# A fused attention and mixing kernel: a third buffer for the weights' raw words, 57 tile slots, and a new order of all steps

## The chip, the cores and the metric

The kernel runs on one core of a Trainium2 chip. The metric is device time in microseconds of the whole program. An engine is named by its short name in the rows: PE is TensorE (and PEld its queue of weight loads), DVE is VectorE, ACT is ScalarE, POOL is GpSimd, and SP is the queue that issues the DMAs.

## The reference, cut to what matters

Three blocks follow one another on 4 batches of 768 positions and 384 channels (8 heads of 48). All inputs are float32.

```python
def _attn_ref(q, k, v, alpha):
    for t in range(S):
        state = alpha[:, :, t, :, None] * state + np.einsum('bhd,bhe->bhde', k[:, :, t], v[:, :, t])
        y[:, :, t] = np.einsum('bhd,bhde->bhe', q[:, :, t], state)

def _moe_ref(x, U, V, w_ch1, w_ch2):          # U 768x32, V 32x768, w_ch1 384x1536
    h = x.transpose(0, 2, 1) @ U @ V
    u = x + h.transpose(0, 2, 1)
    return u + np.maximum(u @ w_ch1, 0.0) @ w_ch2

def _moe2_ref(x, w_theta, w_tok_r, w_tok_i, w_ch):
    theta = x @ w_theta
    zr, zi = x * np.cos(theta), x * np.sin(theta)
    y = np.einsum('ts,bsd->btd', w_tok_r, zr) + np.einsum('ts,bsd->btd', w_tok_i, zi)
    u = x + y
    return u + np.maximum(u @ w_ch, 0.0)
```

## The kernel before

**Attention** is worked off in 16 pairs of heads (4 per batch), each in 6 chunks of 128 positions. A pair's inputs `al`, `kk`, `qq`, `vv` are loaded by `att_load` (L189, L190). `prep_k` and `prep_q` make running products of the decay on DVE (the scans L197 and L206) and multiply them into k and q (L199 and L207, on DVE for pairs 0 to 3 and, with one exception, on POOL from pair 4 on). On PE the pair then passes through `att_pe`: transposes of k (L273, copied out by ACT as `kt`), scores A (L252), increments of the state D (L284), the product within the chunks (L305) and that with the earlier state (L313). For pairs 0 to 3 ACT copies the scores out (L259) and POOL masks them (L260); for the later ones DVE does both (L263). L295 on DVE is the scan over the chunks' states, L315 on ACT copies the result Y to `xp`, and SP moves it into the batch's X by DMA (L373). The squares (L234, L235, on ACT) are sums for a flag that is looked at when the program ends; once they are done, the pair's `al` and `G` are free.

**The second block** first mixes positions through U and V. For batch 0 `rank_columns` does so by blocks of 128 channels, as soon as the pairs of a block are there: transposes (L437), ACT's copy (L438), the product with U (L444), `gc` by ACT and DVE (L448, L449), and then two `lift`s of it: x plus the product with V in PSUM (L420, L421), split into a high and a low part `uh` by ACT and DVE (L158, L159), and X written back (L423). The other batches use `rank` (transposes L391). Then come the layers: `expand` is 9 products of 128x384 (L542 to L544) with `wh` and `wl`, the high and low part of a weight, followed by relu on ACT (L563) and the low part on DVE (L564); `contract` is 9 products into `acc`, two steps behind. The third block has theta, a mixing over positions (L724) and a channel product, from tiles that are made in the same manner.

**Weights** come as 64-bit words. `load64` (L169) brings the raw words into a tile `raw` of the pool `rw`, and `conv` puts float32 together from them in three DVE instructions (L466, L468, L470). For the layers' weights ACT then makes the high part (L481) and DVE the low part (L484), which is left until the next conversion is under way.

**Order.** There is no scheduler: every group of steps is a generator, `ORDER` is a string of letters, and each letter advances one generator by a step. What it issues goes into the engines' queues in this order, and every engine takes its own queue in order. D loads a pair, P prepares one, A is a step of `att_pe`, Q a pair's squares, U the load of U and V, L a step of the layers' weights, 0 to 2 a step of a column of `rank_columns`, K of `rank`, M and N of the layers for the two halves of the positions, T of the third block's weights, X loads X again, H is theta, G mixing, C the channel product, F the flag. A step whose input is missing drives the other generator until it is there.

**Memory.** Tiles of 128x768 live in `SLOTS` slots; a tile takes the slot that became free longest ago (`take`, `done_with`), and the DMA or instruction that first writes it waits for the slot's last reader.

Of the kernel before, what the change touches and what calls it, by code (L numbers as in the profile page):

```python
# [24 lines left out]
NF = FF // 128  # L25
HT = S // 2
RANK = 32
SLOTS = 59
LAG = 2

LATE = 0
# [3 lines left out]


ORDER = """
PAAAAAAQAAPUAAAPAUAAAADPAAUUA0U0UPUAAAALPAA0LALALAP1A01AA1PLL1AA0LAAA22A012L2LA2LLLMMD12ALLLMLMMNNLLNMLNLLNLNL
MLNLLLM1MNQLMNMLNLQLAPNNMLQMLMLLLMLLMMMDMMPNMMDMPMAAAAQDAUAQPANPAUNAAAAAAAQPNPNAADAAAAAAAPNANQAAKKNKKKKPNKKKAA
AAPKAANAAADAAKKNNKMQADMAMQMPMMPMMAK2PMMAAMMAAPDAAKMMMPQMMANAAAAQAPADAAMTMMPALAAQAAATAMKPQMNAMNAMDNKNNPKNKKAAAA  # L40
ADPANPNANQLANTKNAAAAAAPKKNNKTAANKNNAANNNAAA0AKKNNATKLMKTKNKMKNQMMMTMTKKMMNMNKMNKKMMMKKNKMTXKMMMKMNMTKNMMNNNNND
MMMNNNTKNMNNNNKNNNNMLMTMMHMTTMMTNTMTTNNMHHNNNTNMMNHMHNHTNFLTPNHNMHNTTTNMTHLHTNMMLMNHMMTTMNNTTTNMNHTPTNHHXNTTT1
MNNGMGGGNHHHGGHG2TTHTGGGHTHGTGGGGTGGTGGGGHGGGHPHHGGGTTHTGNGGGHGGGGHMLFGGGGGHFGQGGHXHHHGGGHGGGGCCGHGHTGLGCGHGGG
HHGGGHGNPFHGGGG0HGLHGHGGCQAHGGGCGCMH0HGHGGGLGHGGHGGHHGDGGTHHHGGGGCHCGGHGGHGGKHLAHGHCDGLGHGLGHGGGHCGGCHGGGHFHHG
GGGHHGCGGHGGHGHHHGGGGGHFGGGGGHCGGCXGHGCGGHGGHKCHLGCGGGGGXGGCCCCCCHAGGLPCCC
"""


# [14 lines left out]
def linear_attention_moe_kernel(ctx, tc, aT, kT, qT, vP, vT, U, V4, w1, w2, wth, wtr, wti, wch, out):  # L63
# [4 lines left out]
    pools = {}  # L68

    @contextmanager  # L70
    def work(slots, name):
        old = dict(pools)
        with ExitStack() as es:
            pools["big"] = es.enter_context(tc.tile_pool(name=f"big{name}", bufs=slots))
            pools["sml"] = es.enter_context(tc.tile_pool(name=f"sml{name}", bufs=3))
            pools["rw"] = es.enter_context(tc.tile_pool(name=f"rw{name}", bufs=2))
            pools["ps"] = es.enter_context(tc.tile_pool(name=f"ps{name}", bufs=8, space=bass.MemoryType.PSUM))
            yield
        pools.clear()
        pools.update(old)  # L80
# [8 lines left out]

    fast = ExitStack()  # L90
    fast.enter_context(work(SLOTS, "f"))
    dr = ctx.enter_context(tc.tile_pool(name="dr", bufs=1, space=bass.MemoryType.DRAM))


    free, home = {"on": True, "s": list(range(SLOTS)), "p": list(range(8))}, {}

# [9 lines left out]
    def T(name, dt=F32):  # L106
        return take("s", name, 768, dt)
# [4 lines left out]
    def done_with(*ts):  # L112
        for t in ts:
            if t.tensor.name in home:
                kind, i = home.pop(t.tensor.name)
                free[kind].append(i)
# [4 lines left out]
    def two(t):  # L121
        return t.rearrange("p (a b) -> p a b", a=2)
# [29 lines left out]
    def split(src, hi, lo, e_hi=None, e_lo=None):  # L152
        if e_hi is pool:
            pool.tensor_scalar(out=hi, in0=src, scalar1=1.0, scalar2=0.0, op0=ALU.mult, op1=ALU.add)
        elif e_hi is dve:
            dve.tensor_copy(hi, src)
        else:
            act.copy(hi, src)  # L158
        (e_lo or dve).tensor_tensor(out=lo, in0=src, in1=hi.bitcast(F32), op=ALU.subtract)  # L159

    def load64(*srcs):
        r = pools["rw"].tile([128, 1536], I32, tag="raw", name="raw")
        o = 0
        for x in srcs:
            n = x.free_size() * 2
            d = r[:, o:o + n]
            if len(x.shape) == 3:
                d = d.rearrange("p (a b) -> p a b", a=x.shape[1])
            sync.dma_start(d, x.bitcast(I32))  # L169
            o += n  # L170
        return r, o // 2
# [289 lines left out]
    def conv(raw, put):  # L461

        r, n = raw
        lo, hi = (r[:, 0:2 * n].rearrange("p (n t) -> p n t", t=2)[:, :, i] for i in range(2))
        t = T("cv", I32)[:, 0:n]
        dve.tensor_scalar(out=t, in0=hi, scalar1=3, scalar2=0x3FFFFFFF, op0=ALU.logical_shift_left, op1=ALU.bitwise_and)  # L466
        yield n * 0.6
        dve.scalar_tensor_tensor(out=t, in0=hi, scalar=-0x40000000, in1=t, op0=ALU.bitwise_and, op1=ALU.bitwise_or)  # L468
        yield n * 1.25
        dve.scalar_tensor_tensor(out=t, in0=lo, scalar=29, in1=t, op0=ALU.logical_shift_right, op1=ALU.bitwise_or)  # L470
        put(t.bitcast(F32))
        yield n * 1.25

    def load_w12():

        lows = []

        def put(n, W):
            def high(v):
                h, l = T("wh", F32R), T("wl", F32R)  # L480
                act.copy(h, v)  # L481

                def low():
                    (dve if BY_W[n] == "V" else pool).tensor_tensor(out=l, in0=v, in1=h.bitcast(F32), op=ALU.subtract)  # L484
                    done_with(v)
                    W.extend((two(h)[:, i], two(l)[:, i]) for i in range(2))

                lows.append(low)
                load(n + 2)

            return high

        first, second = [[(f, w, W) for f in range(0, NF, 2)] for w, W in ((w1, W1), (w2, W2))]
        todo = first[:1] + [x for y in zip(first[1:], second) for x in y] + second[-1:]
        raws = {}

        def load(n):
            if n < len(todo):
                f, w, W = todo[n]
                raws[n] = load64(w[f:f + 2].rearrange("f p n -> p f n"))  # L500

        for n in range(2):
            load(n)
        yield 0
        for n in range(len(todo)):
            g = conv(raws.pop(n), put(n, todo[n][2]))
            yield next(g)
            yield next(g)
            if lows:
                lows.pop()()  # L510
            yield next(g)
        lows.pop()()
# [110 lines left out]
    def load_second():  # L623
        def by():
            return dve if BY_T[len(WT) + min(len(CH), KD - 1)] == "V" else pool

        def put_thch(v):
            v = two(v)
            pool.tensor_scalar(out=v[:, 0], in0=v[:, 0], scalar1=INV2PI, scalar2=0.0, op0=ALU.mult, op1=ALU.add)
            for i, W in ((0, TH), (1, CH)):  # L630
                t = two(T("wt", F32R))
                split(v[:, i], t[:, 0], t[:, 1], e_lo=by())
                W.append(t)
            done_with(v)

        def put_tok(key):
            def put(v):
                hi, lo = T("wkh", F32R), T("wkl", F32R)
                split(v, hi, lo, e_lo=by())
                done_with(v)  # L640
                WT[key] = (hi, lo)
            return put

        todo = [((wth[j], wch[j]), put_thch) for j in range(KD)]
        todo += [((w[s],), put_tok((n, s))) for s in range(NC) for n, w in (("r", wtr), ("i", wti))]
        raws = {}

        def load(i):
            if i < len(todo):
                raws[i] = load64(*todo[i][0])  # L650

        load(0)
        load(1)
        yield 0
        for i, (_, put) in enumerate(todo):
            yield from conv(raws.pop(i), put)
            load(i + 2)

    def load_x1(b):
        if b < B - 1:  # L660
# [158 lines left out]
    att_load(0, 0)  # L819
    att_load(0, 1)  # L820
    lw, lu = load_w12(), load_uv()
    next(lu)
    att_load(0, 2)
# [132 lines left out]
    def checked():  # L956
        while late or len(done) < B * NP:
# [3 lines left out]
    done, ready = [], [(0, 0)]  # L961
    gens = {"D": loads(), "P": preps(), "A": products(), "Q": squared(), "U": lu, "L": lw, "K": others(),
            "M": layers(0), "N": layers(1), "T": load_second(), "X": back(), "H": angles(), "G": mixing(),
            "C": channels(), "F": checked()}
    gens.update((str(j), mixed(j)) for j in range(KD))
# [7 lines left out]
    with tc.If(fine[0] < 1):  # L973
        xg = dr.tile([B * NP, 96, S], F32, name="xg")
        x1g = dr.tile([B, KD, 128, S], F32, name="x1g")
        with work(1, "ga"):
            att_any(xg)
        flat = xg.rearrange("(b p) c t -> b (p c) t", b=B).rearrange("b (k c) t -> b k c t", k=KD)
        with work(30, "g1"):
            drain(load_uv())  # L980
            W1.clear()
            W2.clear()
            drain(load_w12())
            with tc.For_i(0, B) as i, inner(24, "g2"):
                X["any"] = [T(f"X{j}") for j in range(KD)]
                for j in range(KD):
                    sync.dma_start(X["any"][j], flat[bass.ds(i, 1), j].rearrange("a p t -> (a p) t"))
                drain(rank("any"))
                drain(mlp("any"))
                drain(finish())  # L990
                for j in range(KD):
                    sync.dma_start(x1g[bass.ds(i, 1), j].rearrange("a p t -> (a p) t"), X["any"][j])
# [68 lines left out]
```

## Time and profile before

| what | value |
|---|---|
| time, median of 3 runs | 682.81 us (682.65 to 682.84) |
| time of the profiled execution | 682.58 us |
| its span, first to last instruction | 680.8 us |
| busy: PE, PEld, DVE, ACT, POOL | 661.6, 638.4, 396.9, 250.5, 143.5 us |
| mean granted clock of PE | 0.999 |
| read from HBM, written | 49.40 MB, 8.26 MB |

The span is that of the profiled execution, and busy times are within it. PE is busy for 97% of the span. A busy time counts an instruction from its start to its modelled end, so the drain of one matmul can lie over the start of the next; where the text counts work on PE, it counts from start to start.

### The profile page before, as it was taken

How to read it: one execution, taken by the hardware profiler on the slowest of the kernel's cores; microseconds unless marked ns; L12 is line 12 of the kernel's file. 1: busy time of each engine (PE TensorE's matmuls, PEld its weight loads, DVE VectorE, ACT ScalarE, POOL GpSimd, SP SyncE). 2: the span in 40 equal slices, each digit the busy share in tenths (PEclk: the TensorE clock that was granted, in tenths of full speed). 3: DMA queues.
4: the chain of work that ended last, by engine and by line, in shares of the span. 5: the costliest groups of instructions: out<-in, count | busy, mean ns of one | idle time of the engine just before them, and what ended most of it. 6: DMA issues, size and time to landing. Idle time of an engine off the chain costs nothing.

```text
span 680.8 us, 11581 instructions
## 1 busy us (share of the span) xinstructions
PE 661.6 (97%) x4766; PEld 638.4 (94%) x4766; DVE 396.9 (58%) x615; ACT 250.5 (37%) x519; POOL 143.5 (21%) x123
## 2 busy tenths in 40 slices
PE   6889999999999999999999999999999999999996
PEld 4678999989999999999999999999999999999996
DVE  8998887868656566444333755657642363454233
ACT  3555352542534333242212444323441343244120
POOL 4550012222222132010100412415230121122010
PEclk9999999999999999999999999999999999999999
DMA  8735555333716330250100412412020000000002
GB/s 319 259 125 192 174 172 163 120 107 106 243 37 198 105 106 20 65 186 0 47 1 1 162 48 93 162 48 92 1 70 36 0 36 1 36 24 12 25 36 86
DMA packets 24077, 63.20 MB, mean 93 GB/s; under 512 B 2896, under 2 KB 6864, under 8 KB 24016
## 3 DMA queue, kind: packets, MB, share of 16 engines
q1 hardware_dynamic: 24016, 62.39, 27.6%
q8 instruction: 39, 0.64, 0.4%
q14 instruction: 22, 0.18, 0.1%
HBM read 49.40 MB, written 8.26 MB: 85 GB/s over the span
## 4 chain that ended last, share of the span: by engine, by line
PE 91%; DVE 5%; DMA 1%; issue 1%; POOL 1%; ACT 1%; SPq 0%; DVEq 0%; ACTq 0%; POOLq 0%
PE mx L724 22%; PE acc L542 8%; PE h L542 7%; PE acc L544 7%; PE acc L543 7%; PE h L543 7%; PE h L544 7%; PE Y L313 3%; PE A L252 3%; PE Y L305 3%; PE th L544 2%; PE ch L542 2%; PE ch L544 2%; PE th L542 2%; PE th L543 2%; PE ch L543 2%
## 5 line engine op out<-in xcount | busy, mean ns | idle before, releaser
L564 DVE SCALAR_TENSOR_TENSOR hh<-h,hh 128x384 fp32r<-128x384 f32 x96 | 53.0, 555 | 104.5 <-ACT hh L563 104.3
L542 PE MATMUL acc<-hh,wh 128*128 128x384 f32 x288 | 97.7, 339 | 0.0
L542 PE MATMUL h<-uh,wh 128*128 128x384 f32 x288 | 97.3, 338 | 0.0
L544 PE MATMUL acc<-hh,wl 128*128 128x384 f32 x288 | 96.4, 335 | 0.0
L544 PE MATMUL h<-uh,wl 128*128 128x384 f32 x288 | 96.4, 335 | 0.0
L543 PE MATMUL h<-uh,wh 128*128 128x384 f32 x288 | 96.4, 335 | 0.0
L543 PE MATMUL acc<-hh,wh 128*128 128x384 f32 x288 | 96.3, 335 | 0.0
L563 ACT ACTIVATE hh<-h 128x384 fp32r<-128x384 f32 x96 | 46.7, 490 | 97.9 <-PE h L544 96.8
L724 PE MATMUL mx<-wkh,zh 128*128 128x384 f32 x288 | 74.8, 340 | 0.0
L724 PE MATMUL mx<-wkl,zh 128*128 128x384 f32 x288 | 73.4, 335 | 0.0
L724 PE MATMUL mx<-wkh,zl 128*128 128x384 f32 x288 | 73.2, 335 | 0.0
L542 PEld LDWEIGHTS acc<-hh,wh 128*128 128x128 f32 x288 | 54.1, 188 | 1.0
L542 PEld LDWEIGHTS h<-uh,wh 128*128 128x128 f32 x288 | 54.1, 188 | 0.8
L543 PEld LDWEIGHTS h<-uh,wh 128*128 128x128 f32 x288 | 54.1, 188 | 0.3 <-DVE uh L159 0.3
L543 PEld LDWEIGHTS acc<-hh,wh 128*128 128x128 f32 x288 | 54.1, 188 | 0.0
L544 PEld LDWEIGHTS acc<-hh,wl 128*128 128x128 f32 x288 | 54.1, 188 | 0.0
L544 PEld LDWEIGHTS h<-uh,wl 128*128 128x128 f32 x288 | 54.1, 188 | 0.0
L724 PEld LDWEIGHTS mx<-wkh,zl 128*128 128x128 f32 x288 | 52.1, 188 | 0.0
L724 PEld LDWEIGHTS mx<-wkl,zh 128*128 128x128 f32 x288 | 51.9, 188 | 0.2 <-POOL wkl L159 0.2
L724 PEld LDWEIGHTS mx<-wkh,zh 128*128 128x128 f32 x288 | 50.9, 188 | 0.0
L199 POOL TENSOR_TENSOR kk<-kk,G 128x767 f32<-128x767 f32 x12 | 21.9, 1829 | 111.4 <-DVE G L197 87.5
L691 ACT COPY xc<-x1t 128x384 f32<-128x384 f32 x24 | 11.5, 479 | 82.2 <-PE x1t L685 82.2
(135 smaller groups left out, 1195.5 us busy)
## 6 DMA issues: line engine op xcount, KB each, us to landing
raw<-in_w SPq DMA_DIRECT2D x12, 768.0 KB, 4.4
al<-in_aT SPq DMA_DIRECT2D x15, 384.0 KB, 3.9
kk<-in_kT SPq DMA_DIRECT2D x15, 384.0 KB, 4.3
qq<-in_qT SPq DMA_DIRECT2D x15, 384.0 KB, 5.2
vv<-in_vP SPq DMA_DIRECT2D x16, 291.0 KB, 5.1
raw<-in_wtr SPq DMA_DIRECT2D x6, 768.0 KB, 4.3
raw<-in_wti SPq DMA_DIRECT2D x6, 768.0 KB, 4.4
out<-ot SPq DMA_DIRECT2D x24, 192.0 KB, 1.9
```

Source lines behind the costliest of these rows:

```text
L199: (dve if BY_K[b * NP + p] == "V" else pool).tensor_tensor(out=k[:, x:y - 1], in0=k[:, x:y - 1], in1=G[:, x:y - 1], op=ALU.mult)
L252: pe.matmul(ts[h][:, j * C:(j + 1) * C], k[r, c], q[r, c], start=True, stop=True)
L305: pe.matmul(t[64 * h:64 * h + n, o], v[:, c * 96 + h * D:c * 96 + h * D + n], ms[g][h][:, j], start=(j == 0), stop=(c == 0), skip_group_ch ...
L313: pe.matmul(t[64 * h:64 * h + D, o], st[64 * h:64 * h + 64, :, c - 1], q[64 * h:64 * h + 64, c * C:(c + 1) * C], start=False, stop=True, s ...
L542: pe.matmul(out, a[0], b[0], start=first, stop=False)
L543: pe.matmul(out, a[0], b[1], start=False, stop=False)
L544: pe.matmul(out, a[1], b[0], start=False, stop=last)
L563: act.activation(h[:, 0], t[:, 0:HT], ACTF.Relu)
L564: dve.scalar_tensor_tensor(out=h[:, 1], in0=t[:, 0:HT], scalar=0.0, in1=h[:, 0].bitcast(F32), op0=ALU.max, op1=ALU.subtract)
L691: act.copy(xc, xt[:, 0:DM])
L724: pe.matmul(ACC[b, j][hf][:, 0:HT], z[:, i, c], w[:, hf * HT:(hf + 1) * HT], start=f, stop=l)
```

## The change

Three things. The pool of raw words gets three buffers instead of two in the main part of the program, and both generators that load weights begin three loads ahead instead of two. There are 57 tile slots instead of 59, which pays for the buffer. And `ORDER` is a new string. Every instruction of the program is still there, in the same number on each engine.

```diff
-SLOTS = 59
+SLOTS = 57
...
 ORDER = """
-PAAAAAAQAAPUAAAPAUAAAADPAAUUA0U0UPUAAAALPAA0LALALAP1A01AA1PLL1AA0LAAA22A012L2LA2LLLMMD12ALLLMLMMNNLLNMLNLLNLNL
...
+AAAAPAAAAPAUPUAAAAAAPAAAAU0UUPU0AUAAALQPL0ALADAAA1LPA01AAPLA00A122LLA1AA221122LLMQLALNMNLNAALLALMLLLMLLMMMLLLN
...
-            pools["rw"] = es.enter_context(tc.tile_pool(name=f"rw{name}", bufs=2))
+            pools["rw"] = es.enter_context(tc.tile_pool(name=f"rw{name}", bufs=3 if name == "f" else 2))
...
                 lows.append(low)
-                load(n + 2)
+                load(n + 3)
...
-        for n in range(2):
+        for n in range(3):
             load(n)
...
         load(0)
         load(1)
+        load(2)
         yield 0
         for i, (_, put) in enumerate(todo):
             yield from conv(raws.pop(i), put)
-            load(i + 2)
+            load(i + 3)
```

What this does to the queues is shown at three places. The first is SP's queue after the first copies to X. X_336 (X_342 in the new kernel) and X_472 (X_475) are channel blocks 1 and 2 of batch 0, the copies to them here come from pairs 1 and 2, and al, kk, qq, vv belong to pair 4. Before:

```order
L373 DMA X_336<-xp 48x768
L189 DMA al<-in_aT 128x768
L189 DMA kk<-in_kT 128x768
L189 DMA qq<-in_qT 128x768
L190 DMA vv<-in_vP 128x582
L169 DMA raw<-in_w 128x2x768 x2
L373 DMA X_336<-xp 48x768
L373 DMA X_336<-xp 16x768
L373 DMA X_472<-xp 32x768
L169 DMA raw<-in_w 128x2x768
```

After:

```order
L373 DMA X_342<-xp 48x768
L169 DMA raw<-in_w 128x2x768 x3
L373 DMA X_342<-xp 48x768
L373 DMA X_342<-xp 16x768
L373 DMA X_475<-xp 32x768
L189 DMA al<-in_aT 128x768
L189 DMA kk<-in_kT 128x768
L189 DMA qq<-in_qT 128x768
L190 DMA vv<-in_vP 128x582
L169 DMA raw<-in_w 128x2x768
```

Pair 4's four loads moved from ahead of the raw loads to behind them and behind pair 2's three copies to X, and three raw loads stand together.

The second place is the start of ACT's queue, from pair 0's second copies of the scores to pair 3's `tb`; the two rows of L234 and L235 are pair 0's squares. Before:

```order
L259 COPY Am_84<-A 128x384 x2
L234 ACTIVATE junk,sq<-al 128x768
L235 ACTIVATE junk,sq<-G 128x767
L315 COPY xp<-Y 112x384 x2
L231 COPY tb<-tt 128x288
```

After, the same stretch, and then the place between pair 2's copies of Y and pair 3's `tb`:

```order
L259 COPY Am_84<-A 128x384 x2
L315 COPY xp<-Y 112x384 x2
L231 COPY tb<-tt 128x288
```

```order
L438 COPY xs<-xt 128x384 x2
L315 COPY xp<-Y 112x384 x2
L234 ACTIVATE junk,sq<-al 128x768
L235 ACTIVATE junk,sq<-G 128x767
L231 COPY tb<-tt 128x288
L274 COPY kt<-kT 128x384
L274 COPY kt<-kT 128x256
L259 COPY Am_83<-A 128x384 x2
```

The squares moved from behind pair 0's scores, where they were the only thing to do, to the place ahead of pair 3's `tb`, `kt` and scores.

The third place is PE's queue from the scores of pair 4 on; X_243 (X_241) is channel block 0. Before:

```order
L252 MATMUL A<-qq,kk 128x128 x12
L284 MATMUL D<-vv,kt 64x48 x10
L437 MATMUL xt<-ident,X_472 128x128 x6
L420 MATMUL h<-X_243,ident 128x384
L421 MATMUL h<-v_400,gc 128x384
L420 MATMUL h<-X_336,ident 128x384
L421 MATMUL h<-v_400,gc 128x384
L444 MATMUL g<-xs,uf 128x128 x6
L305 MATMUL Y<-Am_85,vv 64x128
```

After:

```order
L252 MATMUL A<-qq,kk 128x128 x12
L284 MATMUL D<-vv,kt 64x48 x10
L444 MATMUL g<-xs,uf 128x128 x6
L420 MATMUL h<-X_342,ident 128x384
L421 MATMUL h<-v_390,gc 128x384
L420 MATMUL h<-X_342,ident 128x384
L421 MATMUL h<-v_390,gc 128x384
L420 MATMUL h<-X_475,ident 128x384
L421 MATMUL h<-v_390,gc 128x384
L420 MATMUL h<-X_475,ident 128x384
L421 MATMUL h<-v_390,gc 128x384
L542 MATMUL h_721<-uh,wh 128x384
```

The transposes L437 and two lifts now stand ahead of pair 4's scores, the four other lifts follow one another, and h_721 is the first of five expands that come before pair 4's L305; in the kernel before there were two expands between L305 and L313, with two lifts behind them.

## Rows read from the trace of the kernel before

**Rows 1.** Busy time by stretch (us from start; engines' us, instructions; clock; DMA share, GB/s).

```profile
25.00:65.00 40.00, 34.53 (x367) 28.05 (x364) 36.88 (x50) 21.37 (x50) 16.34 (x13) 1.00 0.52 174
65.00:675.00 610.00, 609.29 (x4202) 596.06 (x4200) 337.97 (x530) 218.10 (x445) 117.39 (x82) 1.00 0.24 80
```

**Rows 2.** TensorE's waits: line, releaser: us in total, times, longest us.

```profile
PE Y L305 <- POOL Am L260: 2.6, 5, 0.9
PE xt L437 <- DMA X<-xp: 2.1, 2, 1.6
```

**Rows 3.** Who waited for the tile raw, whole run (us, times).

```profile
  DVE cv L466: 0.3, 1
```

**Rows 4.** SP's queue in time: start us, us, instruction, count.

```profile
25.99 0.58 SPq L189 DMA_DIRECT2D al<-in_aT  x1
...
34.83 1.79 SPq L373 DMA_DIRECT2D X<-xp  x3
```

**Rows 5.** DMA issues: count, KB each, us to landing (page; X at 140 to 148 us).

```profile
al<-in_aT SPq DMA_DIRECT2D x15, 384.0 KB, 3.9
...
X<-xp SPq DMA_DIRECT2D x2, 144.0 KB, 2.8
```

**Rows 6.** VectorE in time: start us, us, instruction, count [idle before <-releaser].

```profile
13.84 1.76 DVE L206 TENSOR_TENSOR_SCAN al<-al,starts 128x768 f32<-128x768 f32 x1
...
35.99 0.57 DVE L466 TENSOR_SCALAR cv<-raw 128x768 int32<-128x768 int32 x1 [0.30 <-DMA raw<-in_w]
...
38.66 2.06 DVE L197 TENSOR_TENSOR_SCAN G<-al,ends 128x767 f32<-128x767 f32 x1
...
40.94 0.76 DVE L295 TENSOR_TENSOR_SCAN S<-D,tb 128x288 f32<-128x288 f32 x1
41.73 0.30 DVE L449 TENSOR_TENSOR gc<-g,gc 32x128 fp32r<-32x128 f32 x1
...
42.29 2.63 DVE L206 TENSOR_TENSOR_SCAN al<-al,starts 128x768 f32<-128x768 f32 x1
...
63.94 0.95 DVE L484 TENSOR_TENSOR wl<-cv,wh 128x768 fp32r<-128x768 f32 x1
```

**Rows 7.** ScalarE in time.

```profile
12.29 0.89 ACT L234 ACTIVATE junk<-al 128x768 bf16<-128x768 f32 x1
...
14.06 0.19 ACT L235 ACTIVATION_READ_ACCUMULATOR junk<-G 128x1 f32 x1
...
36.75 1.64 ACT L259 COPY Am<-A 128x384 f32<-128x384 f32 x4
...
55.36 0.48 ACT L423 COPY X<-h 128x384 f32<-128x384 f32 x1 [0.62 <-DVE uh L159]
```

**Rows 8.** POOL in time.

```profile
37.38 4.14 POOL L260 TENSOR_SCALAR_AFFINE_SELECT Am<-Am 128x384 f32<-128x384 f32 x4 [1.72 <-ACT Am L259]
41.49 1.81 POOL L199 TENSOR_TENSOR kk<-kk,G 128x767 f32<-128x767 f32 x1
44.99 2.13 POOL L207 TENSOR_TENSOR qq<-qq,al 128x768 f32<-128x768 f32 x1 [1.69 <-DVE tt L228]
```

**Rows 9.** TensorE in time, 25 to 70 us.

```profile
42.35 1.34 PE L313 MATMUL Y<-qq,S 64*48 64x128 f32 x20
...
65.05 0.34 PE L544 MATMUL acc<-hh,wl 128*128 128x384 f32 x1
```

**Rows 10.** Busy time in one stretch, columns as in the first group.

```profile
42.35:64.70 22.35, 21.23 (x189) 17.32 (x189) 19.99 (x30) 11.10 (x26) 3.08 (x2) 1.00 0.33 107
```

**Rows 11.** TensorE in time, 138 to 150 us.

```profile
140.54 1.33 PE L313 MATMUL Y<-qq,S 64*48 64x128 f32 x20
...
147.53 1.03 PE L391 MATMUL xt<-ident,X 128*128 128x128 f32 x6 [0.19 <-DVE Am L263]
```

**Rows 12.** ScalarE in time, 138 to 150 us.

```profile
141.92 0.48 ACT L315 COPY xp<-Y 112x384 f32<-112x384 f32 x1 [0.18 <-PE Y L313]
```

**Rows 13.** The queue of TensorE's weight loads: waits, us, times, longest us.

```profile
PEld Y L313 <- DVE S L295: 2.5, 8, 0.5
```

More of the change, by code (lines that the diff above doesn't have):

```diff
@@ L37 @@
 ORDER = """
-PAAAAAAQAAPUAAAPAUAAAADPAAUUA0U0UPUAAAALPAA0LALALAP1A01AA1PLL1AA0LAAA22A012L2LA2LLLMMD12ALLLMLMMNNLLNMLNLLNLNL
[L39 to L45, printed above, removed]
+AAAAPAAAAPAUPUAAAAAAPAAAAU0UUPU0AUAAALQPL0ALADAAA1LPA01AAPLA00A122LLA1AA221122LLMQLALNMNLNAALLALMLLLMLLMMMLLLN
+L0MMLMLNMLQMNLLLDNNLLNMLMLLNLMLMMMTMLPMMNMPAMDMPNAANQAAAQUANDPAPNAAAAAAQQADNUAPAPAAAAAQAAPNNKKNKKKKAKDKAAKAAQP
+AKKNNANPDNLAKADNMMPMMAUAAAAPAPLMAAMK1M2QAQAAAAKMMDAPMPMAMMMAAAKMMMAAAAAMPAAAQAAAQKAKDMKAPMMPMMMKTKNKQAKNDNAAAA
+AKPKNPDLNNNPNQTANNAKANNNPKNNNNNTNQNAA2AAAAAATKNKMMAAAAXAKAMNTUKMNAKMDMKNMKNMTPNMNMTKMKKMKMNNKPTNNKNNNNKNNTMKLM
+NTMKMTNMMMKNNMFUMMNFTTMMMMFNNKTQNDNMMMNNKMMHMHNNNHNMTNTHNNTMHNNNTMNTNMMTAHMMMMKTNT0MTMHLTMNNHHTTTTMMMNQXTNTNHG
+NTTGNTLNGNLHNT1GNHGTGGGHTGHTGHTMHGTXHGHAKHATGTGGGNHGMGGHGTGXGTGTHTGGGHGHGGXMGGHGUHPGFHGNGGGTGGHHCPGCGHGCGGCHQC
+FGGGHLGHGAHGGGLGGHGHHHGHGG0GGHGGGGHHTHLGGCGGGGGHHGHGGHHKGHDGHGGGGTGCCGGHHHGGGCHHHGGGHGHG1HHGCLGDGGHGCGGGGPHGLG
+LHGHGGHGCGNF2HGHGGHCGHGLGLGGGHGGGHGLCGGHGGCPGGXHHHGGGHGGGHGHGHGHCGGGGGGGGGGFCCH0GCCGCHCGCCHCLCC
 """
```

## The prediction, made before the changed kernel was run

> **What bounds the kernel now.** I read the table by stretches first: TensorE's busy time, then how busy the other engines are while it idles [rows 1]. From 65 to 675 us it is busy for 609.29 of 610 us, at a granted clock of 1.00; from 25 to 65 us it loses 5.47 us (40.00 - 34.53). (Before 25 us the order of the engines that it waits for is the same in both kernels.) VectorE (DVE) is busy 36.88 of those 40 us, so this short stretch, in which it prepares attention and converts the weights' 64-bit words, is where an order of steps can matter; after it the new order can only damage what is full. The list of TensorE's waits names what it misses: masked scores from POOL, 2.6 us in five waits, and the landing of X, 2.1 us in two [rows 2]. The weights' raw words are hardly missed: over the whole run one wait of 0.3 us, by VectorE [rows 3]. That is the whole direct worth of a third raw buffer.
>
> **The queue of loads.** In the kernel before, SP issues pair 4's four loads at 25.99 us, ahead of two raw loads and of pair 2's copies to X at 34.83 us [rows 4]. The order shows al behind three raw loads and behind those three copies. The copies' time is set by pair 2's Y, which the change leaves where it was: the first 57 rows of VectorE are the same in both. So al goes out at 34.83 + 1.79 = 36.6 us, and lands by the page's 3.9 us [rows 5] at 40.5; the raw loads have landed by then, so I take 40.1 to 40.6. VectorE wants it in L197, which ran at 38.66; without the 0.30 us wait for raw [rows 6] it could at 38.4. The idle time is 40.1 - 38.4 = 1.7 us. Behind L197 in VectorE's queue stands L295, the scan that gives pair 3's states: before it ended at 40.94 + 0.76 = 41.7, now at 40.1 + 2.06 + 0.2 + 0.76 = 43.1.
>
> **The squares.** Pair 0's two squares ran from 12.29 to 14.06 + 0.19 = 14.25 us on ScalarE (ACT), 1.96 us in time in which nothing else was ready [rows 7]. They now stand between pair 2's copies of Y and pair 3's `tb`. That place had 0.98 us of idle, so what comes behind it, above all the score copies of L259 (36.75 us), is about 1.1 us later (1.96 less 0.98, and 0.1 for the additional switches). POOL's four selects, 4.14 us from 37.38 [rows 8], follow: 38.5 to 42.6, and L305, which reads them, ends at 43.4 and not at 42.35 (the start of L313 [rows 9]). The two delays meet at the same L313 and don't add: **+1.05 us** there; with al at 40.6 instead, 43.6 and +1.25. Undisturbed by either it would be 0.
>
> **From there to the expands.** Before, 22.35 us pass from that L313 to the first contract step, of which TensorE is busy for 21.23 [rows 10]; a block's last matmul drains while the next begins, and counted from start to start the 18 blocks in that window (42.35 and 65.05 are their ends [rows 9]) hold 19.95 us of work. So 2.40 us are lost, 1.12 of it plainly idle. After, the same stretch up to the end of the fifth expand holds three expands more by 2 (2 x 1.57) and not yet pair 4's L305 and L313 (1.46 + 1.27): 19.95 + 3.13 - 2.73 = 20.35 us. What waits there now: the transposes L437 for X's landing (L313's end, two copies of 0.48, the issue, and 2.8 us to land [rows 5]: about 48.4, when the work put ahead of it ends too, so 0 to 0.3); then four lifts in a row. A lift passes ScalarE, VectorE and ScalarE again, with 0.62 us of wait inside [rows 7], about 1.5 us each against 0.81 on TensorE, and the first expand needs the last of them: 1.4 us. With 0.3 of switches the loss is 1.6 to 1.7: **-0.7 us** (0 if lifts and X each cost 0.4 more; -1.3 if the lifts overlap better).
>
> **Where the weights are just in time.** Before, the low part of the first contract's weights ends at 63.94 + 0.95 = 64.89 [rows 6] and is read at 65.05 [rows 9]: 0.16 us of room. After, this step has some 3 us, but the contracts then come in longer runs, and following the letters one later weight has a lead of 10.5 us of TensorE's work where its conversions need 10.6. I take **+0.3** (0 to 1).
>
> **Rank of batch 1.** Pair 7's L313 starts at 140.54; its copies end at 142.40 [rows 11, 12], the DMAs land about 2.8 + 0.5 later [rows 5], at 145.7. Before, about 5.5 us of other products lie between L313's end at 141.8 and the first L391, which starts at 147.53 and waits 0.19 for VectorE. In the new order only one expand and one contract lie there, 3.3 us; the landing is 3.8 after L313's end. **+0.45** (0 to 0.8).
>
> **Attention in the full stretch.** Where L313 follows directly on its own L305, its weights wait for the scan: 2.5 us in eight places, 0.31 each [rows 13]. The new order has such neighbours 8 times where there were 10: **-0.6** (0 to -0.8).
>
> **At nothing:** the third raw buffer (0.3 us, used up by the wait for al); 57 slots (in both orders loads find a slot free before the data is wanted, and VectorE has room from 100 us on; uncovered, a load late by its 3.9 us costs that at one place); the order of mixing and channel products, fed by steps that are ready several products ahead.
>
> Sum: 1.05 - 0.7 + 0.3 + 0.45 - 0.6 = +0.5 us. The profiled execution took 682.58 (span 680.8 and 1.8 around it), so 683.1; the median of the runs shown, 682.81, is 0.23 above it: **683.3 us**.
>
> **A rule that bears on VectorE.** L206 took 2.63 us while POOL's product of k ran, 41.49 to 43.30 [rows 8]; the same scan with nothing on POOL took 1.76 us at 13.84 [rows 6]. In the new order VectorE's two L159 of the first lifts stand just where POOL multiplies q (2.13 us [rows 8]). If they too were held until POOL is done, VectorE would be 1.05 us later for the masks, gc and lifts behind: 684.4. I take them as not held, since L449, which like them has one operand in PSUM, took its 0.30 us at 41.73 beside the same POOL product [rows 6]. The Trainium skill, "SBUF — State Buffer", section "Who interferes with whom", says that a VectorE instruction with two SBUF inputs contends with a GpSimd instruction that reads SBUF, and one with at most one such input, outside the two-port modes, doesn't; by it the sum stays 683.3.
>
> **Rivals and chances.** (1) *As summed*, 681.9 to 684.1: 0.43. (2) *The weights come late*, slower. The six L159 and late al put VectorE behind in 48 to 60 us, and it is the engine that makes every weight. One conversion takes 2.7 us (35.99 to 38.66 [rows 6]); if VectorE ends one conversion behind where contracts run through without expands, the sum grows by up to 2.7: 684.2 to 687. It decides once the lag at 60 us is over the room of the just-in-time weight, about 0. For it: VectorE's 36.88 of 40 us. Against: before, it catches up by 70 us, and the third raw buffer lets it convert back to back. 0.25. (3) *POOL holds L159*: 684.4, 0.08. (4) *Faster*: the squares find ScalarE idle for longer than 0.98 us or al lands by 39, so L313 loses 0.3, and the lifts overlap, since VectorE has all four in one run, so the 2.40 us fall to 0.8: 0.3 - 1.6 + 0.15 - 0.45 = -1.6, hence 681.2; with rank hidden, 680.5. For it: the early expands stand where TensorE idles. Against: VectorE makes their operands. 0.20. (5) *The change does nothing*: loads are hidden either way and delays of 1 us vanish in waits further on: 682.8, 0.04.
>
> A measurement of this kernel can tell about 0.2%, 1.4 us, from no change. Faster than 681.4 is (4): 0.20; same is (1) and (5): 0.47; slower than 684.2 is (2) and (3): 0.33. The range leaves out the best part of (4) and the worst of (2): 680.9 to 686.2.
>
> **What would show it.** In the new trace: al for pair 4 issued at 36.6 and VectorE idle 1.7 us before L197, released by that DMA; no wait for raw; squares between 34.8 and 36.8 on ScalarE; pair 3's L313 at 43.4; a wait of TensorE for uh of about 1.4 us ahead of the first expand's last products; TensorE's first L391 waiting 0.45 us for X; TensorE's loss in 65 to 675 us under 1.5 us. The prediction is wrong if al lands before VectorE asks, if TensorE waits for wl or wh between 65 and 100 us by more than 1 us, or if waits show up after 150 us, where I cost the order at nothing.

## The result, and the profile after

The changed kernel takes 688.31 us (median of 4 executions, 687.64 to 690.77), the one before 682.83: ratio 1.0085, 95% interval 1.0073 to 1.0097. It is slower by 5.5 us, outside the predicted range of 680.9 to 686.2. The profiled execution took 687.64 with a span of 685.9, 5.1 us more than before.

TensorE's busy time by stretch, with the columns of [rows 1]:

```profile
25.00:65.00 40.00, 34.34 (x346) 29.01 (x345) 32.71 (x48) 24.97 (x60) 14.18 (x13) 1.00 0.52 161
65.00:680.00 615.00, 611.30 (x4227) 595.07 (x4223) 341.69 (x532) 217.95 (x441) 118.25 (x82) 1.00 0.24 80
```

Start-up loses about what it lost before (5.66 of 40 us, before 5.47). The stretch behind it, full before but for 0.71 us of 610, now has 3.70 us idle in 615. TensorE's list of waits, as in [rows 2], names most of that:

```profile
PE Y L313 <- DVE S L295: 1.9, 1, 1.9
PE Y L305 <- POOL Am L260: 1.8, 3, 0.9
...
PE h L542 <- DVE xs L159: 1.2, 1, 1.2
...
PE xt L437 <- DMA X<-xp: 0.9, 2, 0.5
PE th L544 <- POOL x1s L159: 0.8, 2, 0.5
PE xt L391 <- DMA X<-xp: 0.6, 1, 0.6
PE D L284 <- DVE hh L564: 0.5, 1, 0.5
```

The names in a row are of the waiting tile and of the tile whose writing or reading ended the wait. `h <- xs`, `th <- x1s`, `xt L391 <- X` and `D <- hh` are waits after 100 us, and none of these had a row before. In start-up the wait for X at L437 has shrunk (2.1 before) and one for the states S has come (1.9). What led there, on SP, VectorE, POOL and TensorE, answering to [rows 4, 6, 8, 9]:

```profile
26.06 1.69 SPq L169 DMA_DIRECT2D raw<-in_w  x3
34.91 1.79 SPq L373 DMA_DIRECT2D X<-xp  x3
36.74 0.59 SPq L189 DMA_DIRECT2D al<-in_aT  x1
```

```profile
40.12 1.75 DVE L197 TENSOR_TENSOR_SCAN G<-al,ends 128x767 f32<-128x767 f32 x1 [1.89 <-DMA al<-in_aT]
...
42.09 0.76 DVE L295 TENSOR_TENSOR_SCAN S<-D,tb 128x288 f32<-128x288 f32 x1
```

```profile
38.16 1.94 POOL L260 TENSOR_SCALAR_AFFINE_SELECT Am<-Am 128x384 f32<-128x384 f32 x4 [2.42 <-ACT Am L259]
```

```profile
38.99 2.02 PE L305 MATMUL Y<-Am,vv 128*64 128x128 f32 x24
42.90 1.34 PE L313 MATMUL Y<-qq,S 64*48 64x128 f32 x20 [1.89 <-DVE S L295]
...
64.70 1.52 PE L305 MATMUL Y<-Am,vv 128*64 128x128 f32 x24
```

al goes out at 36.74 us behind the raw loads and the copies to X, VectorE waits 1.89 us for it, and the states for L313 come at 42.85. The five expands are over at 64.70, where L305 starts. Counted as in the prediction, these 21.80 us from the start of L313 hold 20.35 us of work, so 1.45 us are lost, where the kernel before lost 2.40. L313 starts 0.55 us later, so the changed kernel is 0.4 us *ahead* at 65 us. All of the 5.1 us, and 0.4 more, is lost behind this point.

Four places can be named. First, TensorE around 144 us, where batch 1's transposes meet X's landing ([rows 11] before). From the first of them to the next product 1.35 us pass (143.28 to 144.63), before 0.78 (147.53 to 148.31): 0.6 us.

```profile
143.28 0.38 PE L391 MATMUL xt<-ident,X 128*128 128x128 f32 x2
144.25 0.63 PE L391 MATMUL xt<-ident,X 128*128 128x128 f32 x4 [0.59 <-DMA X<-xp]
```

Second, all engines from 166 to 178 us: the copies of batch 0's X to memory (x1d), and what stands behind them.

```profile
166.25 1.34 SPq L615 DMA_DIRECT2D x1d<-X  x3
...
171.27 1.75 DVE L197 TENSOR_TENSOR_SCAN G<-al,ends 128x767 f32<-128x767 f32 x1 [1.73 <-DMA x1d<-X]
...
172.18 0.49 ACT L563 ACTIVATE hh<-h 128x384 fp32r<-128x384 f32 x1 [3.23 <-DMA x1d<-X]
...
173.53 0.79 PE L284 MATMUL D<-vv,kt 128*64 128x48 f32 x20 [0.45 <-DVE hh L564]
...
174.15 2.14 PE L305 MATMUL Y<-Am,vv 128*64 128x128 f32 x24
```

VectorE's scan and ScalarE's relu sit idle for 1.73 and 3.23 us, released by the DMA of x1d: their output tiles were given slots that X had held and that the copy still reads. D and L305 follow late. D waits 0.45 us for L564, the low part of a relu, which had to queue up behind these; its `hh` is not an operand of D, but L564 is the last reader of the `h` in the PSUM bank that D takes over. L305 takes 2.14 us where 1.5 is usual: 1.1 us in all.

Third, all engines around 294 us:

```profile
293.46 0.49 PE L391 MATMUL xt<-ident,X 128*128 128x128 f32 x3
293.98 0.48 ACT L158 CAST xs<-xt 128x384 fp32r<-128x384 f32 x1 [2.23 <-PE xt L391]
294.49 0.56 DVE L159 TENSOR_TENSOR xs<-xt,xs 128x384 fp32r<-128x384 f32 x1 [2.15 <-ACT xs L158]
...
295.11 0.45 PE L542 MATMUL h<-uh,wh 128*128 128x384 f32 x1 [1.16 <-DVE xs L159]
```

An expand waits 1.16 us for VectorE to have read `xt`, which is not its operand; from the transposes to it pass 1.65 us, and 0.24 from the transposes to the next product where nothing waits (the run with the rank step, below): 1.4 us.

Fourth, around 482 us, where theta's products wait for POOL's splits:

```profile
478.95 4.81 POOL L159 TENSOR_TENSOR x1s<-Y,x1s 128x384 fp32r<-128x384 f32 x3 [5.71 <-ACT x1s L158]
...
481.23 0.33 PE L542 MATMUL th<-wt,x1s 128*128 128x384 f32 x1
...
482.53 0.44 PE L544 MATMUL th<-wt,x1s 128*128 128x384 f32 x1 [0.27 <-POOL x1s L159]
...
483.81 0.44 PE L544 MATMUL th<-wt,x1s 128*128 128x384 f32 x1 [0.48 <-POOL x1s L159]
...
484.09 0.49 PE L686 MATMUL x1t<-ident,Y 128*128 128x128 f32 x3
```

Nine products take 2.86 us (481.23 to 484.09) and not 1.57: 1.3 us.

### The profile page after: what moved, and what is told of

Its sections match the earlier page's. It is cut to its first block, busy times and chain, and to the rows that moved or that the text cites. A ratio compares the mean times of both kernels' runs of the same rounds, so it can differ in the third digit from the quotient of the medians.

```text
span 685.9 us, 11587 instructions
## 1 busy us (share of the span) xinstructions
PE 664.0 (97%) x4766; PEld 638.8 (93%) x4766; DVE 396.4 (58%) x615; ACT 252.1 (37%) x519; POOL 141.7 (21%) x123
## 4 chain that ended last, share of the span: by engine, by line
PE 79%; DVE 7%; issue 5%; POOL 3%; DMA 3%; ACT 2%; SPq 0%; POOLq 0%; DVEq 0%; ACTq 0%
PE mx L725 18%; PE h L542 7%; PE h L543 7%; PE h L544 7%; PE acc L542 6%; PE acc L543 6%; PE acc L544 6%; PE Y L305 3%; PE A L252 3%; PE Y L313 2%; PE ch L544 2%; PE ch L542 2%; PE ch L543 2%; PE th L544 2%; PE th L543 2%
## 5 line engine op out<-in xcount | busy, mean ns | idle before, releaser
L564 DVE SCALAR_TENSOR_TENSOR hh<-h,hh 128x384 fp32r<-128x384 f32 x96 | 52.9, 555 | 105.6 <-ACT hh L563 104.1
L159 POOL TENSOR_TENSOR wkl<-cv,wkh 128x768 fp32r<-128x768 f32 x12 | 22.8, 1903 | 86.3 <-ACT wkh L158 86.3
```

The lines of the kernel that those rows point to most:

```text
L564: dve.scalar_tensor_tensor(out=h[:, 1], in0=t[:, 0:HT], scalar=0.0, in1=h[:, 0].bitcast(F32), op0=ALU.max, op1=ALU.subtract)
```

## The experiments

The theory after the result: the new order loses time at single places behind 100 us, the two slots fewer cost at one of them, and start-up is not to blame. Rivals: the loss is the slots' alone; or it is the start-up's, by loads that come late for the rest.

**Order, buffers and slots apart.** The new order with everything else as before:

```diff
 SLOTS = 59          # and bufs=2, load(n + 2), load(i + 2), as before
-PAAAAAAQAAPUAAAPAUAAAADPAAUUA0U0UPUAAAALPAA0LALALAP1A01AA1PLL1AA0L...
+AAAAPAAAAPAUPUAAAAAAPAAAAU0UUPU0AUAAALQPL0ALADAAA1LPA01AAPLA00A122...
```

> The new order alone: two raw buffers, loads two ahead and 59 slots, as in the kernel before. If the 5 us are lost by the order itself, at single places after 100 us: 687 to 689 us, as the whole change. If they are lost because 57 slots are too few, so that tiles wait for slots whose last reader is a DMA: at most 684 us. If the third raw buffer is worth something, this is slower than the whole change; I expect 0 to 0.5 us of that.

Measured 687.97 us (686.97 to 689.80): the loss is there with all 59 slots, so it is not the slots' alone. But the sentence on the third buffer was wrong. Who waited for `raw`, and TensorE's waits from 60 to 100 us:

```profile
  DVE cv L466: 5.3, 5
```

```profile
PE h L542 <- DVE hh L564: 1.2, 1, 1.2
```

With two buffers VectorE waits 5.3 us for raw words in this order (0.3 in the old one, none with three), and an expand waits 1.2 us for an `hh` that VectorE then makes late, again not as its operand but for a PSUM bank; in the changed kernel TensorE is busy for 35.00 of 35 us from 65 to 100. Nothing in this trace waits for x1d, and the time is that of the changed kernel all the same.

Traces of kernels that differ in slots, buffers and loads alone list the same products in the same sequence (and where one step of TensorE's is moved, all but a few), so they can be compared product by product. Against the changed kernel's trace this one loses 1.8 us from 66 to 100 us and wins back 0.9 from 170 to 180: the missing buffer takes what the two slots give, and more. (It is the slowest of the four executions, and 1.0 of its loss falls from 43 to 50 us, see the clock below.)

**The third buffer with the old order.** 59 slots and three buffers fit when the squares write over their inputs and the three gc tiles become one:

```diff
-            act.activation(junk, a, ACTF.Square, accum_out=sq[:, i, 0:1])
+            act.activation(a, a, ACTF.Square, accum_out=sq[:, i, 0:1])
...
-        gt = pools["sml"].tile([128, 128], F32R, tag="gc", name="gc")
+        if "gc" not in late_gc:
+            late_gc["gc"] = pools["sml"].tile([128, 384], F32R, tag="gt", name="gt", bufs=1)
+        gt = late_gc["gc"][:, j * 128:(j + 1) * 128]
```

> The old order and 59 slots with the third raw buffer and loads three ahead. Memory for it comes from the squares, which write over their inputs (dead by then) instead of into a tile of their own, and from gc, whose three tiles are pieces of one. If a third raw load ahead of pair 2's copies to X makes them land late (3.8 MB in front of them instead of 3.0): TensorE waits about 3 us for X near 40 us instead of 1.6, and the time is 1 to 2.5 us over the kernel before, with the granted clock under 1.00 near 45 us. If the buffer is harmless with the old order: 682.3 to 683.0.

Measured 684.25 us (682.51 to 688.04), ratio 1.0033 (1.0007 to 1.0059): slower, with executions 5.5 us apart. TensorE at the transposes that waited 1.59 us in the kernel before (L436 in this kernel is L437 there):

```profile
41.27 1.33 PE L436 MATMUL xt<-ident,X 128*128 128x128 f32 x6 [3.71 <-DMA X<-xp]
```

The second run begins only two loads at first, and the third and fourth behind the first conversion:

```diff
-        for n in range(3):
+        for n in range(2):
             load(n)
...
-                load(n + 3)
+                for m in ((2, 3) if n == 0 else (n + 3,)):
+                    load(m)
```

> As the run before this, with the third raw load begun behind pair 2's copies to X. If only its place in the queue hurts: 682.2 to 682.9, as the kernel before (its one wait of 0.3 us for raw words is all that there is to gain, and that wait is for the first load, so it may stay).

Measured 682.62 us (682.46 to 683.10), ratio 0.9999 (0.9990 to 1.0009), as expected. The buffer is worth nothing to the old order, and costs 1.5 us there in the median if its load stands ahead of the copies to X.

**Which stretch.** Two orders were cut at 100 us and joined crosswise, with two buffers and 59 slots: the first letters of the one, then the other without the letters already used.

> The first 141 letters of the new order (to about 100 us), then the old order without the letters already used; two raw buffers and 59 slots. If the new start-up is not what costs, as the traces show (0.3 us ahead of the kernel before at 64.7 to 100 us): 682.3 to 682.9 us. If the start-up costs later, by an order of loads that hurts afterwards: 684 us or more.

> The first 139 letters of the old order (to about 100 us), then the new one without the letters already used; two raw buffers and 59 slots. If the order after 100 us costs the 5 us: 687 to 689 us. If the start-up or the slots cost them: at most 684 us.

The old start with the new rest takes 686.56 us, 3.8 over the kernel before, so the rest loses most, as expected (687 to 689 was a little high, for 59 slots). The new start with the old rest takes 684.93, not 682.3 to 682.9: I had left out that this start needs the third buffer. Its VectorE waits 5.3 us for raw words here too, and an expand waits 1.2 us at 81 us, as above. A second part is the clock: in this trace the first expand starts at 57.23 us (56.08 in the changed kernel), at a granted clock of 0.70 from 45 to 50 us. Behind 100 us TensorE waits 0.4 us in all, as in the kernel before.

**The start-up's queue of loads.** One letter of the changed kernel moved:

```diff
-...U0UUPU0AUAAALQPL0ALADAAA1LPA01...
+...U0UUPU0AUAAADLQPL0ALAAAA1LPA01...
```

> The changed kernel with one letter moved: pair 4's loads go out ahead of the three raw loads and of pair 2's copies to X, as before. The wait of 1.9 us of VectorE for al and that of TensorE for the states (1.89 us at 42.9) should go. If the time of the end follows from it: 686.4 to 687.3 us, that is 1 to 1.9 us less than the changed kernel. If the lifts or the copies to X take the gain back: within 0.5 us of the changed kernel.

Measured 689.21 us (688.71 to 690.42), 0.9 more than the changed kernel, where 1 to 1.9 less was expected. VectorE no longer waits for al, but TensorE waits 3.08 us for pair 2's X, whose copies are issued from 34.8 us, as before, and have landed 6.4 us later (SP's queue, then TensorE in time):

```profile
28.02 1.62 SPq L169 DMA_DIRECT2D raw<-in_w  x3
34.77 1.96 SPq L373 DMA_DIRECT2D X<-xp  x3
```

```profile
41.22 1.30 PE L437 MATMUL xt<-ident,X 128*128 128x128 f32 x6 [3.08 <-DMA X<-xp]
```

Ahead of these copies stand, by the page's sizes, 2.3 MB of raw loads in the changed kernel (no wait for X there), pair 4's 1.4 MB and two raw loads, 3.0 MB, in the kernel before (a wait of 1.59), and all of it, 3.7 MB, here (the expectations say 3.8). So the late al was the price of the third raw load. The next run has pair 4 early and the third load late:

> As the run with pair 4's loads early, but the third raw load is begun behind pair 2's copies to X, so that 3.0 MB and not 3.8 MB stand ahead of these. If the copies landed late there (41.2 us) because the third raw load was in front of them: X lands at about 39.2 as in the kernel before, TensorE waits 1.0 to 1.6 us for it and not 3.1, L313 of pair 3 starts at about 42.0 (42.9 in the changed kernel), and the time is 0.5 to 1.0 us under the changed kernel's. If the copies wait for pair 4's loads and not for the raw load: X lands at 41 again and the time is that of the early loads, 689.2.

```profile
39.17 0.84 PE L437 MATMUL xt<-ident,X 128*128 128x128 f32 x6 [0.85 <-DMA X<-xp]
40.35 2.28 PE L305 MATMUL Y<-Am,vv 128*64 128x128 f32 x24 [0.34 <-POOL Am L260]
42.56 1.34 PE L313 MATMUL Y<-qq,S 64*48 64x128 f32 x20
```

Measured 686.47 us (685.75 to 686.63), 1.8 under the changed kernel's first median, more than expected. But the start is only a part of it: X lands at 39.2, and L313 starts at 42.56, not at the 42.0 of the expectation. Product by product against the changed kernel's trace, 0.45 of some 2.0 us are gained up to 66 us. Another 0.9 comes at 174 us, where D waits for nothing in this trace, and 0.7 at 144 and 482 us: places that the edit does not touch, and whose waits vary between traces, as the next runs show.

**Slots.** One slot more, which fits without other changes:

> The changed kernel with 58 slots instead of 57, nothing else. If tiles near 171 us wait for slots whose last reader is the copy of X to memory (ScalarE 3.23 us and VectorE 1.73 us there, TensorE about 1.1 us at L284 and L305): these waits shrink or go, and the time is 0.5 to 1.3 us under the changed kernel's 688.3. If the waits there come from the order of steps, not from the slots: no change, and the same two waits in the trace.

Measured 688.13 us (686.23 to 689.21): not told apart. The relu's wait for x1d is still there (2.84 us). With 59 slots, three buffers and the new order, and the changed kernel measured beside it:

> The changed kernel with 59 slots and nothing else of its order or buffers changed (memory found as in the runs of the old order with three buffers). If 57 slots cost by waits for slots that a copy of X still reads: no such wait near 170 us, and 0.4 to 1.3 us under the changed kernel of the same call. If that wait costs TensorE nothing on average: within 0.4 us.

> The changed kernel itself once more, for more executions. If the lower granted clock after the wait near 42 us takes part in what was lost: the executions spread over 687 to 691 us again, with the fewest at 687.6. If the first spread was chance: all within 0.5 us.

The changed kernel took 687.83 us (686.50 to 690.24) and this one 687.36 (686.70 to 688.01): the medians don't settle it. The traces do: with 59 slots nothing waits for x1d, and TensorE's stretch from 100 to 200 us reads, changed kernel first,

```profile
100.00:200.00 100.00, 97.54 (x915) 90.01 (x914) 69.84 (x116) 40.93 (x93) 29.59 (x14) 1.00 0.46 148
```

```profile
100.00:200.00 100.00, 99.23 (x931) 92.45 (x929) 71.45 (x118) 40.45 (x94) 29.72 (x14) 1.00 0.47 150
```

2.46 us idle against 0.77, of which 1.4 is L284 behind a late hh. How late the copy of X lands varies, and with it this loss: L284's wait reads 0.5 and 1.4 us in the two traces of the changed kernel, 1.0 in that of a later run, and nothing in four others with 57 slots and the same stretch. In the three that wait, the copies x1d took 5.4, 6.3 and 6.0 us to landing; in the four others 4.2 to 5.1.

**The rank step at 294 us.** One letter moved ahead by two places:

```diff
-...AMNTUKMNAKMDMKNMK...
+...AMNTUKMKNAMDMKNMK...
```

> The changed kernel with one letter moved: the step of batch 3's rank that stands at 293.5 us comes one contract (nine products) earlier, so that a contract and not an expand follows it. If the expand waits there because it has to take the PSUM bank of the transposes just issued, which VectorE reads last (1.16 us idle, 1.4 us lost): the wait goes and the time is 1.2 to 1.5 us under the changed kernel's. If it waits for VectorE being late in general: the wait moves and the time stays within 0.4 us.

```profile
292.13 0.49 PE L391 MATMUL xt<-ident,X 128*128 128x128 f32 x3
292.37 0.42 PE L542 MATMUL acc<-hh,wh 128*128 128x384 f32 x1
...
294.04 0.33 PE L542 MATMUL h<-uh,wh 128*128 128x384 f32 x1
```

Measured 686.12 us (685.15 to 687.75), 2.2 under the changed kernel's first median, where 1.2 to 1.5 was expected; not all of that is this place. Product by product against the changed kernel's trace, 1.4 us are gained from 290 to 300 us, the expected size. The wait is gone: a contract, which needs no new bank, follows the transposes, and the expand starts on time. In `take`'s bookkeeping two halves' `acc` and `g` hold seven of the eight PSUM banks there; the expand gets the one that `xt` has just left.

**Theta's splits at 481 us.** First the splits two mixing steps earlier, then the products two later:

```diff
-...NHGMGGHGTGXGTGTHTGGGH...
+...NHGMHGGGTGXGTGTHTGGGH...    # theta_split_earlier
+...NHGMGGHGTGXGTGTTGGHGH...    # theta_later
```

> The changed kernel with one letter moved: the step that splits X for theta at 477 us comes two mixing steps (2.1 us of TensorE) earlier. If theta's products wait only since POOL's three splits (1.6 us each) begin 2.3 us ahead of the first product: TensorE's waits of 0.27 and 0.48 us there go, and the time is 0.9 to 1.3 us under the changed kernel's. If POOL is the bound there, or a product of mixing is then late: within 0.4 us.

```profile
482.39 0.45 PE L544 MATMUL th<-wt,x1s 128*128 128x384 f32 x1 [0.60 <-POOL x1s L159]
```

Measured 687.57 us, and TensorE still waits 0.60 us, as it does in the trace of the rank-step run without this change: ScalarE makes the high parts behind `zh`, which waits for its own inputs, so the splits didn't come earlier against the products. The splits begin 2.29 us ahead of the first product, as without the change (2.28). This run decides nothing.

> The changed kernel with theta's products at 481 us put two mixing steps (2.1 us) later, instead of its splits earlier. If POOL's splits are what they wait for: no wait for x1s there, and 0.8 to 1.3 us under the changed kernel of the same call, provided that the mixing steps put ahead find their operands. If these steps wait instead: within 0.4 us.

Measured 686.99 us (685.82 to 688.13) beside 687.83 of the changed kernel. No wait for x1s is left, and TensorE's idle time from 400 to 500 us goes from 0.61 to 0.00 us. It was POOL's splits. The gain in the median, 0.8, lies within the spreads; product by product it is 1.3 us against the changed kernel's first trace and 0.9 against the second, all from 480 to 490 us.

**The clock.** The changed kernel's ten executions spread over 4.3 us. The same 10 us in the changed kernel's profile and in that of the kernel with 58 slots (TensorE's busy time and granted clock from 40 to 50 us, then TensorE's first expand):

```profile
40.00:45.00 5.00, 3.07 (x36) 2.29 (x34) 4.67 (x6) 1.79 (x5) 1.91 (x2) 1.00 0.97 309
45.00:50.00 5.00, 4.65 (x44) 4.02 (x44) 3.67 (x8) 3.27 (x9) 2.13 (x1) 1.00 0.28 78
```

```profile
40.00:45.00 5.00, 3.07 (x35) 2.25 (x33) 4.67 (x6) 1.78 (x5) 1.91 (x2) 0.91 0.93 313
45.00:50.00 5.00, 5.00 (x29) 4.00 (x27) 3.23 (x8) 3.01 (x8) 2.13 (x1) 0.75 0.26 73
```

```profile
56.08 0.34 PE L542 MATMUL h<-uh,wh 128*128 128x384 f32 x1
```

```profile
57.16 0.34 PE L542 MATMUL h<-uh,wh 128*128 128x384 f32 x1
```

In both L313 starts at 42.90 after 1.89 us of idle TensorE. In one the granted clock is then 0.91 and 0.75, a mean of its two levels of 1.2 and 2.4 GHz, and the first expand starts 1.08 us later. Of nine traces with this wait (1.7 to 1.9 us) five show such a fall, and 14.3 us from L313 to the first expand; in the four others it is 13.2 to 13.4. So the wait for al costs a second time in some executions. Where the granted clock fell from 30 to 35 us instead, pair 3's L313 was not late by it: with 0.66 in the old order with the late third load it started at 42.36, in the kernel before at 42.35.

Neither trace of the changed kernel itself shows the fall at 42.9. Its second trace (688.69 us, 1.05 over the first) has 0.66 from 30 to 35 us, but what it lost more is D's longer wait at 174 us, 1.0 us. So the clock is one part of the spread and the landing of x1d another; the two slowest executions (690.24 and 690.77) have no trace, and what slowed them is not shown.

**Put together.** The new order with all repairs, one expand put ahead of batch 1's first rank steps, and 58 slots; and the repaired start with the old rest, with three buffers and 59 slots.

> The new order with all repairs that were made one by one (pair 4's loads early, the third raw load late, the rank step and theta's splits earlier), one expand put ahead of batch 1's first two rank steps, and 58 slots. If the losses add up as they were found (0.45 at the start, 1.4, 0.4, about 0.5): 684.5 to 685.3. If repairing one place moves the wait to the next: over 685.7.

> The new order's start to about 100 us with pair 4's loads early and the third raw load late, then the old order; three raw buffers, 59 slots (memory found as in the two runs before). In the run with those two repairs alone TensorE was 0.75 us ahead of the kernel before from 70 to 138 us. If all that was lost is in the new order after 100 us: 681.8 to 682.2, faster than both kernels. If the old rest needs the old start: 683 or more.

The first takes 684.47 us (684.03 to 685.80), just under the expected stretch, though not each part of that sum came: in its trace theta's products still wait, 0.3 and 0.5 us, and where the transposes of batch 1 waited for X a product behind them now waits 0.3 us for VectorE. It stays 1.8 us over the kernel before, and this rest was not taken apart. The second takes 681.76 us (681.42 to 682.00), ratio 0.9985 (0.9976 to 0.9994): 0.9 us under the kernel before and 6.5 under the changed one.

```profile
25.00:65.00 40.00, 35.13 (x357) 29.61 (x355) 34.76 (x50) 25.41 (x60) 15.76 (x13) 1.00 0.53 165
65.00:675.00 610.00, 608.77 (x4220) 594.97 (x4215) 339.12 (x532) 214.17 (x439) 117.56 (x82) 1.00 0.24 81
```

TensorE is busy for 35.13 of 40 us in start-up, where it was 34.53 before. From 102 us on its trace lists the products of the kernel before in the same sequence, the first 0.72 us earlier and the last ones 0.8: the gain is the start's.

## Why the prediction was wrong

**What failed** is the paragraph "At nothing", in two of its three parts. *The order of mixing and channel products, "fed by steps that are ready several products ahead"*: theta's products at 481 us were not: 1.3 us. The same paragraph had nothing on the rank steps of batch 3, where a PSUM bank, not an operand, is what the expand waits for: 1.4 us. *57 slots, "loads find a slot free before the data is wanted"*: I looked at loads, but the tiles that ScalarE and VectorE write wait too, for a slot that the copy of X still reads: 1.1 us in the profile. With batch 1's transposes (0.6 over before), these are 4.4 of the 5.5 us lost behind 65 us. The other 1.1 us lies in waits of 0.2 to 0.4 us, among them xs at 148 and 150 us, qq at 213 and masked scores at L305; it was not taken apart.

Term by term, forecast and found in the profile: L313 +1.05 and +0.55; from there to the expands -0.7 and -0.95; weights +0.3 and 0; batch 1's rank +0.45 and +0.6; attention's neighbours -0.6 and about 0; "at nothing" 0 and +3.8; not taken apart +1.1. That is +0.5 and +5.1 us. The median of the runs is another 0.7 us above the profile. The lower clock after the wait at 42.9 (1.1 us where it shows) and D's varying wait (up to 1.0 us more) have that size; neither was foreseen, and the share of each is not shown.

**The queue of loads**: right. al at 36.7 (36.6 said), 1.9 us of idle VectorE (1.7), the states at 42.85 (43.1).

**The squares**: wrong. The term for L313 was +1.05 and is +0.55, and the states at 42.85 alone made it. The squares did make L259 0.8 us late, but POOL's four selects took 1.94 us and not 4.14 [rows 8], so L305 was done at 41.0. VectorE was waiting for al just then (idle from 38.23 to 40.12). Where it works meanwhile, the selects take 3.49 us (pair 4 early, third load late). The Trainium skill, "SBUF — State Buffer", section "Who interferes with whom", has VectorE's instructions with two SBUF inputs and GpSimd's reads contend for a shared port pair. The selects agree: 1.94 us beside an idle VectorE and 3.49 beside its conversion and scan, which read two SBUF tiles each (L470: raw and cv; L197: al and ends). It is the same rule that I had weighed for L159 alone.

**From there to the expands**: right in kind, -0.95 against -0.7. The weight loads of the first expand's last products wait 0.35 and 0.41 us for uh, where 1.4 in all was said: the lifts were priced too high. With L313 0.55 late the start is 0.4 us ahead where the sum had +0.35.

**Weights just in time** (+0.3): no wait from 65 to 100 us. **The third buffer at nothing**: right for the old order, as measured, wrong for the new, whose start it carries.

**Rank of batch 1** (+0.45): a wait of 0.59 us, right. **Attention's neighbours** (-0.6): TensorE's weight loads wait 1.9 us in six places for the states from 100 to 600 us, before 2.5 in eight. But the weight loads also sit idle for some 0.2 us before an L313 where the profile names nothing that they wait for (1.1 us in five places, before 0.4 in two), so their idle time before L313 is 3.0 us in all, before 3.1. And a new 1.2 us in five waits, for the masked scores at L305 (0.5 of it in the second place above), comes on top. What a neighbour costs had been read from the waits with a name alone.

**The rivals**: none had the mechanism. The changed kernel's 688.3 lies above even the slowest. The slower one put the loss in late weights, which never came late, and the prediction named waits after 150 us as what would make it wrong; it gave them no price.

## What to carry to other kernels

Where one engine is full, a new order can win only in the stretch that is not, and lose everywhere: so walk each change of neighbours in the full stretch, for the operands, the PSUM bank and the slot that each step takes, not only the stretch where the gain is. A buffer is worth what the order makes of it: the third one was worth nothing to the old order, and let the new start go without 5.3 us of VectorE's waits, but only with its load behind the small copies that others wait for. When parts of a change go opposite ways, joining one stretch of each order shows it; with the start's loads repaired as well it gave the fastest kernel here. And where kernels list the same products in the same sequence, comparing their traces product by product tells what one place is worth, where medians of executions that spread over 4 us cannot.

## What was not expected of the hardware

Three small copies to X, issued from 34.8 us on, had landed at about 41.2 us with 3.7 MB of loads in front of them and at about 39.2 with 3.0. POOL's select of a 128x384 tile took 0.48 us beside an idle VectorE and 0.87 to 1.03 beside a busy one. After TensorE had been idle for 1.7 to 1.9 us at 41 to 43 us, the granted clock fell in five of nine traces and cost 1.1 us; the kernel with waits of at most 0.95 us there stayed within 0.6 us over eleven executions. The copies of X to memory at 166 us (384 KB each) took 4.2 us to landing in one trace and 6.3 in another of the same order; ScalarE and VectorE, waiting for the slots that these copies still read, sat idle for 0.6 to 3.8 us.
